# Reordering the values and the transposes of a fused sketch-attention and expert-attention kernel

## The chip, the cores and the metric

The kernel runs on one core of a Trainium2 chip. The metric is the device time of one execution in microseconds. A core has TensorE (PE, the matmuls; PEld are its weight loads), VectorE (DVE), ScalarE (ACT), GpSimd (POOL) and SyncE (SP, here only a DMA queue).

## The reference

Two blocks, one after the other. The first is a linear attention with 4 heads over 1088 positions and 4 batches; its output, 4 x 32 wide, is the input `x` (4, 1088, 128) of the second:

```python
phi(x) = outer(S1 @ x, S2 @ x)              # 8 * 8 = 64 features per head
x = (phi(q) @ (phi(k).T @ v)) / (phi(q) @ phi(k).sum() + 1e-6)

logits = x @ w_gate                          # 4 experts, the best 2 are kept, softmax over them
for e in range(4):
    q, k, v = x @ wq[e], x @ wk[e], x @ wv[e]         # 64 wide
    a = softmax(causal(q @ k.T / 8))                  # 1088 x 1088
    out += gate[:, e] * (a @ v @ wo[e])               # 0 for the experts not kept
```

Everything is fp32.

## The kernel before, in words

Per batch, `prepare` computes `x` and projects it: sketches (`kps`, `qps`), products on GpSimd (`kp`, `qp`), `kv`, turned features (`tq`), numerators (`num`), turned `x` (`tx`), values with gate logits (`vg`), queries and keys (`qk`, `qkt`). It is cut into pieces. Those of batch b+1 wait in the queue `fill` and are let out a few at a time by `spend` between the steps of batch b, so that PE has other work there. The fourth batch has no fill.

The expert attention of a batch goes by steps. One step is one tile of 128 query rows with one pair of experts: tile i (0 to 7) has 128(i+1) keys, and the pair g is 0 or 1. Two tiles 2p and 2p+1 of one pair are a group; its two steps are called its first and its second here. The last 64 query rows, with both pairs at once, are the last unit (`scores_last`). The order of groups is p = 0, 1, 2, 3, each with both pairs, then the last unit; in the fourth batch p = 3, the last unit, then p = 2, 1, 0.

A step does this. `scores` (L391) writes the scores of the two experts and adds the causal mask (L394); for more than 512 keys each expert takes a whole buffer of `ps_sc` (two buffers of two banks). VectorE takes the maxima (L401, or L398 for both at once), ScalarE the exponentials with their sums (L377). `turns_of` gives a list of jobs, each of which turns up to four 128 x 128 blocks of the exponentials on PE (L446) into one bank and copies it to `aT` (`evacuate`, every third copy on VectorE, L71, the others on ScalarE, L73). A list for tile i has ceil((i+1)/2) jobs.

At a group's end `gates` makes 1/sum on VectorE (L458, L459) and `rb`, gate weight times 1/sum, on GpSimd (L462); later PE turns `rb` (`rt`, L469) and ScalarE copies it to `rs`. The values (`av`, L511; L548 in the last unit) need the group's whole `aT`. `av` times `rs` gives `yT` (L521), and when both pairs are done `output` projects it (`po`, L567) and stores it.

PE's order is the order in which the program is written (`manual_schedule` for PE). The orders of the other engines come from a scheduler. Of the eight PSUM banks `ps_sc` has four, `ps_tp` three (turns, `rt`, `po`, all of `prepare`, one small score tile of the last unit), and `ps_o` one (`av`, and the other small score tile). A pool's buffers are given out in turn, so a tile waits until the one as many places before it has been read.

The main loop runs step n so: scores of its tile; the turns of the tile before, with fill between; at the last gap the oldest entry of `later`; then, if the tile before closed a group, `close`: gates, and the first half of that group's values. The second half, with `rt` ahead, is an entry of `later` and so falls in the next step:

```python
turn = gates(name, z, gw[:, 2 * p : 2 * p + 2, 2 * g : 2 * g + 2], 256)
values(0, p + 1)
def rest():
    rs = turn()
    values(p + 1, 2 * p + 2)
```

In the last unit's step the turns come first, then its scores and three doses of fill, then `close` of the group before.

## Time and profile before

| what | number |
|---|---|
| median of 3 runs | 468.26 us (466.32 to 468.36) |
| the profiled execution | 466.51 us, span of its core 464.7 us |
| busy: PE, PEld | 406.0 us, 266.7 us |
| busy: DVE, ACT, POOL | 232.7 us, 224.5 us, 63.4 us |
| chain that ended last | PE 68%, DVE 16%, ACT 9% |
| granted TensorE clock, mean | 0.986 of full speed |

The span runs from the first to the last instruction of the core. Matmuls are pipelined and their ends are modelled, so the busy time of PE is not PE at its peak. "Idle before" is the idle time of an engine just before a group of instructions, with the instruction that ended it.

### The profile page before, as it was taken

To read this page: it belongs to the slowest core of one execution; us is meant where nothing else is said; L and a number is where in the kernel's file an instruction comes from. 1 tells how busy PE (TensorE), PEld (TensorE's weight loads), DVE (VectorE), ACT (ScalarE), POOL (GpSimd) and SP (SyncE) were. 2 spreads that over 40 slices of the span, in tenths; PEclk is the share of its full clock that TensorE was granted. 3 is DMA by queue.
4 is the path that set the end of the run, shared out by engine and by line. 5 is a ranking of instruction groups with operands and counts; after the bars stand their busy time and mean duration, and the time that the engine had idled before them with its cause. 6 is when DMAs were issued, how large, how long until landed. Compare 5 with 4: busy or idle time off the path is not lost.

```text
span 464.7 us, 8178 instructions
## 1 busy us (share of the span) xinstructions
PE 406.0 (87%) x3264; PEld 266.7 (57%) x3264; DVE 232.7 (50%) x495; ACT 224.5 (48%) x564; POOL 63.4 (14%) x99
## 2 busy tenths in 40 slices
PE   0579989998996999999898999989899899699995
PEld 0574665764553676675554676765455465366653
DVE  3673754654553355545636344555364535434542
ACT  1124554545454345545645445545445545435652
POOL 4230172000000036000000027000000000000100
PEclk9999999999998999999999999999999999899997
DMA  7450031000000000000000000000000000000000
GB/s 209 126 146 1 1 105 54 1 11 1 11 2 1 13 4 13 0 13 2 0 13 1 1 16 13 2 11 1 1 12 1 0 13 4 0 1 16 1 13 23
DMA packets 11510, 9.98 MB, mean 21 GB/s; under 512 B 3792, under 2 KB 10448, under 8 KB 11472
## 3 DMA queue, kind: packets, MB, share of 16 engines
q1 hardware_dynamic: 9280, 8.92, 6.7%
q10 hardware_dynamic: 2064, 0.53, 0.5%
q8 instruction: 25, 0.41, 0.4%
q14 instruction: 13, 0.11, 0.1%
q0 software_dynamic: 128, 0.01, 0.0%
HBM read 7.23 MB, written 2.23 MB: 20 GB/s over the span
## 4 chain that ended last, share of the span: by engine, by line
PE 68%; DVE 16%; ACT 9%; issue 3%; DMA 2%; POOL 1%; ACTq 0%; DVEq 0%
PE sc L391 16%; PE av L511 15%; PE tp L446 10%; DVE mx L401 6%; ACT a L377 5%; PE qk L313 4%; PE po L567 3%; PE num L288 3%; PE sc L394 3%; PE av L548 2%; DVE aT L71 2%; PE vg L325 2%; DVE mx L429 2%; PE kps L236 2%; PE rt L469 2%
## 5 line engine op out<-in xcount | busy, mean ns | idle before, releaser
L73 ACT COPY aT<-tp 128x512 f32<-128x512 f32 (+1 forms) x119 | 63.5, 542 | 127.6 <-PE tp L446 127.5
L377 ACT ACTIVATE a<-sc,mx 128x1024 f32<-128x1024 f32 (+7 forms) x136 | 103.0, 763 | 36.8 <-DVE mx L431 14.2
L446 PE MATMUL tp<-ident,a 128*128 128x128 f32 (+1 forms) x648 | 98.6, 277 | 5.7 <-DVE vt L71 1.8
L401 DVE TENSOR_REDUCE mx<-sc 128x1 f32<-128x640 f32 (+3 forms) x64 | 62.6, 1019 | 69.8 <-PE sc L394 69.7
L511 PE MATMUL av<-aT,vt 128*64 128x256 f32 (+1 forms) x640 | 80.6, 381 | 13.1 <-ACT a L377 11.6
L446 PEld LDWEIGHTS tp<-ident,a 128*128 128x128 f32 (+1 forms) x648 | 70.8, 141 | 22.4 <-issue 7.4
L391 PE MATMUL sc<-qkT 64*128 64x512 f32 (+3 forms) x384 | 82.6, 518 | 0.0
L462 POOL TENSOR_TENSOR rb<-gw,r 128x256 f32<-128x256 f32 (+1 forms) x36 | 21.2, 588 | 362.7 <-DVE r L459 289.5
L511 PEld LDWEIGHTS av<-aT,vt 128*64 128x64 f32 x640 | 42.0, 140 | 40.3 <-ACT a L377 12.8
L391 PEld LDWEIGHTS sc<-qkT 64*128 64x128 f32 x384 | 33.1, 185 | 36.3 <-issue 31.4
L71 DVE COPY aT<-tp 128x512 f32<-128x512 f32 (+2 forms) x61 | 38.7, 640 | 14.6 <-PE tp L446 14.5
L398 DVE TENSOR_REDUCE mx<-sc 128x2 f32<-128x256 f32 (+3 forms) x32 | 26.3, 822 | 30.3 <-PE sc L394 29.8
L313 PE MATMUL qk<-xT,wqk 128*128 128x512 f32 x64 | 32.4, 603 | 0.8 <-ACT xT L73 0.8
L377 ACT ACTIVATION_READ_ACCUMULATOR a<-sc,mx 128x1 f32 x136 | 27.4, 201 | 0.0
L325 PE MATMUL vg<-wvg,xT 128*128 128x260 f32 (+1 forms) x72 | 21.9, 400 | 4.8 <-DVE aT L71 2.2
L236 PE MATMUL kps<-SKW,kT 128*128 128x128 f32 x72 | 12.1, 320 | 14.2 <-DVE SKW L163 14.2
L521 DVE TENSOR_TENSOR yT<-av,rs 128x256 f32<-128x256 f32 x32 | 13.4, 420 | 21.1 <-PE av L511 20.9
L567 PE MATMUL po<-wo,yT 128*128 128x128 f32 (+1 forms) x144 | 21.7, 293 | 2.3 <-DVE aT L71 1.1
L394 PEld LDWEIGHTS <-identb 128*128 128x128 bf16 x128 | 7.3, 97 | 28.1 <-issue 26.2
L567 PEld LDWEIGHTS po<-wo,yT 128*128 128x128 f32 (+1 forms) x144 | 18.2, 192 | 6.3 <-DVE aT L71 1.9
L236 PEld LDWEIGHTS kps<-SKW,kT 128*128 128x128 f32 x72 | 10.6, 226 | 15.1 <-DVE SKW L163 14.2
L469 PE MATMUL rt<-ident,rb 128*128 128x128 f32 x68 | 13.7, 279 | 5.5 <-DVE aT L71 2.4
(117 smaller groups left out, 409.0 us busy)
## 6 DMA issues: line engine op xcount, KB each, us to landing
kin<-in_k_dram SPq DMA_DIRECT2D x4, 544.0 KB, 3.7
qin<-in_q_dram SPq DMA_DIRECT2D x4, 544.0 KB, 6.0
vin<-in_v_dram SPq DMA_DIRECT2D x16, 128.0 KB, 2.8
out_dram<-ob SPq DMA_DIRECT2D x16, 128.0 KB, 1.8
wqk<-in_moe_wq_dram ACTq DMA_DIRECT2D x1, 128.0 KB, 5.1
wqk<-in_moe_wk_dram ACTq DMA_DIRECT2D x1, 128.0 KB, 5.1
wvg<-in_moe_wv_dram ACTq DMA_DIRECT2D x1, 128.0 KB, 3.3
wo<-in_moe_wo_dram ACTq DMA_DIRECT2D x1, 128.0 KB
```

The costliest lines, as they stand in the source:

```text
L71: nc.vector.tensor_copy(out_, in_)
L73: nc.scalar.copy(out_, in_)
L236: nc.tensor.matmul(t[:, w * (j - j0) : w * (j - j0) + w], xT_[:, 128 * j : 128 * j + 128], SKW.rearrange("p s x h r -> p (s x h r)"), star ...
L313: nc.tensor.matmul(t, wt(a), xT[:, 512 * c : 512 * c + 512], start=True, stop=True)
L325: nc.tensor.matmul(t[0:m, 0 : E * HD + E], xT[:, 128 * j : 128 * j + m], wvg, start=True, stop=True)
L377: nc.scalar.activation(out=dst, in_=src, func=ACTF.Exp, bias=mx, accum_out=z)
L391: nc.tensor.matmul(sc[e][:, c0:c1], qk[rows, g, 128 * i : 128 * i + 128], qk[rows, NG + g, c0:c1], start=True, stop=(c1 < n))
L398: nc.vector.tensor_reduce(mx, t[:, :, 0:n], axis=AX.X, op=ALU.max, negate=True)
L401: nc.vector.tensor_reduce(mx[:, e : e + 1], sc[e][:, 0:n], axis=AX.X, op=ALU.max, negate=True)
L446: nc.tensor.transpose(tp[0:nk, k - k0, :], ats[e][:, 128 * j : 128 * j + nk], ident)
L511: nc.tensor.matmul(av[HD * e : HD * e + HD, lo:256], vt[:, j, c : c + HD], aT[:, 2 * j + e, lo:256], start=(j == 0), stop=(j == 2 * p + 1))
L567: nc.tensor.matmul(po[0:nq, DM * x : DM * x + DM], yT[:, g, 128 * x : 128 * x + nq], wo_sb[:, g], start=(g == 0), stop=(g == NG - 1))
```

## The change

It does three things.

1. `ps_o` is gone and `ps_tp` has four banks. `av` and both small score tiles of the last unit come out of it.
2. The values of a group are one piece, issued right behind the scores of the next group's second tile (in the last unit's step: behind its scores). The turn of the gates, `rt`, is a job of the next group's first step, after the turns and `output`.
3. Where a tile has more than two jobs of turns (tiles 4 to 7), the first half is issued at the end of the tile's own step, and only the rest in the next step.

The doses of fill differ with it: 1.4 shares in a group's first step, 0.6 in its second and 2.4 in the last unit's, of 19 shares a batch, where each step had one of 16 (and 1.5 in the last unit's). The core of the diff:

```diff
-    ps_tp = ctx.enter_context(tc.tile_pool(name="ps_tp", bufs=3, space=bass.MemoryType.PSUM))
-    ps_o = ctx.enter_context(tc.tile_pool(name="ps_o", bufs=1, space=bass.MemoryType.PSUM))
+    ps_tp = ctx.enter_context(tc.tile_pool(name="ps_tp", bufs=4, space=bass.MemoryType.PSUM))
...
-        ext = [ps_o.tile([128, 512], F32, tag="o", name=f"ext{b}_0"), ps_tp.tile([128, 512], F32, tag="tp", name=f"ext{b}_1")]
+        ext = [ps_tp.tile([128, 512], F32, tag="tp", name=f"ext{b}_{e}") for e in range(2)]
...
-                def values(j0, j1, p=p, g=g, aT=aT, yT=yT, name=name, box=[]):
-                    if j0 == 0:
-                        box[:] = [ps_o.tile([128, 512], F32, tag="o", name=f"av{name}")]
-                    av = box[0]
-                    for j in range(j0, j1):
+                def values(rs, p=p, g=g, aT=aT, yT=yT, name=name):
+                    av = ps_tp.tile([128, 512], F32, tag="tp", name=f"av{name}")
+                    for j in range(2 * p + 2):
...
-                def close(p=p, g=g, yT=yT, z=z, name=name, values=values):
-                    turn = gates(name, z, gw[:, 2 * p : 2 * p + 2, 2 * g : 2 * g + 2], 256)
-                    values(0, p + 1)
-                    def rest():
-                        rs = turn()
-                        values(p + 1, 2 * p + 2)
-                        av = values.__defaults__[-1][0]
-                        nc.vector.tensor_tensor(out=yT[:, g], in0=av[:, 0:256], in1=rs, op=ALU.mult)
-                        if g == NG - 1:
-                            later.append(lambda: output(b, p, yT))
-                    later.append(rest)
+                    nc.vector.tensor_tensor(out=yT[:, g], in0=av[:, 0:256], in1=rs, op=ALU.mult)
+                    return (lambda: output(b, p, yT)) if g == NG - 1 else None
+
+                def close(p=p, g=g, z=z, name=name, values=values):
+                    return gates(name, z, gw[:, 2 * p : 2 * p + 2, 2 * g : 2 * g + 2], 256), values
...
-            share = sum(c for c, _ in fill) / (2 * NJ)
...
+            share = sum(c for c, _ in fill) / 19.0
+            for n, (kind, make, turned, close) in enumerate(units(b, *now)):
+                jobs, turns = turns, []
+                if done:
+                    jobs.append(done)
+                    done = None
...
+                    if kind == "A":
+                        box = []
+                        jobs.append(lambda gate_turn=gate_turn, box=box: box.append(gate_turn()))
+                if kind == "L":
+                    for f in jobs:
+                        f()
+                    values = gate_turn()
                     ats = make()
...
+                    done = values()
+                    group = None
+                    for _ in range(4):
+                        spend(share * 2.4 / 4)
+                else:
+                    ats = make()
+                    if kind == "B" and group:
+                        done = group()
+                        group = None
+                    us = share * (1.4 if kind == "A" else 0.6)
+                    gaps = max(len(jobs), 2)
+                    for s in range(gaps):
+                        if s < len(jobs):
+                            jobs[s]()
+                        spend(us / gaps)
+                    if kind == "A" and group:
+                        group = box[0]
...
+                turns = turned(ats)
+                if len(turns) > 2 and kind != "L":
+                    for f in turns[: len(turns) // 2]:
+                        f()
+                    turns = turns[len(turns) // 2 :]
+                if close:
+                    group = close()
```

`kind` is "A" for a group's first step, "B" for its second and "L" for the last unit's.

In the instructions the names end in a number of the buffer; ahead of it stand the batch (0 to 3), the tile or group, the pair, and for `tp` the first block. Line numbers of the changed kernel are one smaller, three at the values, and up to 16 further down. The first place is PE in the last unit of the second batch. Before:

```order
L313 MATMUL qk2_2_0_2336<-xT2_1355,wqk_163 128x512
L414 MATMUL sc1_8_0_2339<-qkT1_371 64x512 x2
L414 MATMUL sc1_8_1_2340<-qkT1_371 64x512 x2
...
L414 MATMUL ext1_0_2341<-qkT1_371 64x64 x2
L414 MATMUL ext1_1_2342<-qkT1_371 64x64 x2
...
L313 MATMUL qk2_1_0_2377<-xT2_1355,wqk_163 128x512
L313 MATMUL qk2_3_0_2380<-xT2_1355,wqk_163 128x512
L511 MATMUL av1_3_1_2388<-aT1_3_1_2155,vt1_160 64x256 x8
L391 MATMUL sc2_0_0_2405<-qkT2_1356 128x128 x2
```

And in the change:

```order
L468 MATMUL rt1_3_1_2307<-ident_139,rb1_3_1_2290 128x128 x2
L413 MATMUL sc1_8_0_2312<-qkT1_368 64x512 x2
L413 MATMUL sc1_8_1_2313<-qkT1_368 64x512 x2
...
L413 MATMUL ext1_0_2314<-qkT1_368 64x64 x2
L413 MATMUL ext1_1_2315<-qkT1_368 64x64 x2
...
L508 MATMUL av1_3_1_2350<-aT1_3_1_2163,vt1_157 64x256 x14
L508 MATMUL av1_3_1_2350<-aT1_3_1_2163,vt1_157 64x128 x2
L324 MATMUL vg2_6_2368<-wvg_161,xT2_1371 128x260
L324 MATMUL vg2_7_2371<-wvg_161,xT2_1371 128x260
L324 MATMUL vg2_8_2374<-wvg_161,xT2_1371 64x260
L312 MATMUL qk2_0_0_2396<-xT2_1371,wqk_160 128x512
```

The whole values of the group before, and its turned gates, stand in this step now; the fill is behind them.

The second place is PE in a group's first step, tile 6 of the second pair, from its scores to those of tile 7. Before:

```order
L391 MATMUL sc1_6_1_1_2158<-qkT1_371 128x384
...
L446 MATMUL tp1_3_0_1_0_2172<-ident_142,a1_7_0_0_2106 128x128
...
L446 MATMUL tp1_3_0_1_8_2187<-ident_142,a1_7_0_0_2106 128x128
...
L567 MATMUL po1_2_2196<-wo_165,yT1_2_1791 128x128 x4
...
L446 MATMUL tp1_3_0_1_12_2204<-ident_142,a1_7_0_0_2106 128x128
...
L511 MATMUL av1_3_0_2218<-aT1_3_0_2045,vt1_160 64x256 x8
L391 MATMUL sc1_7_1_0_2227<-qkT1_371 128x512
```

And in the change:

```order
L390 MATMUL sc1_6_1_1_2166<-qkT1_368 128x384
...
L445 MATMUL tp1_3_0_1_8_2180<-ident_139,a1_7_0_0_2113 128x128
...
L324 MATMUL vg2_1_2186<-wvg_161,xT2_1371 128x260
L445 MATMUL tp1_3_0_1_12_2189<-ident_139,a1_7_0_0_2113 128x128
...
L324 MATMUL vg2_2_2195<-wvg_161,xT2_1371 128x260
L551 MATMUL po1_2_2198<-wo_162,yT1_2_1793 128x128 x4
L324 MATMUL vg2_3_2206<-wvg_161,xT2_1371 128x260
L468 MATMUL rt1_3_0_2209<-ident_139,rb1_3_0_2161 128x128 x2
L324 MATMUL vg2_4_2214<-wvg_161,xT2_1371 128x260
L445 MATMUL tp1_3_1_0_0_2217<-ident_139,a1_6_1_0_2174 128x128
...
L390 MATMUL sc1_7_1_0_2229<-qkT1_368 128x512
```

The step turns the second half of tile 7 of the first pair, then the first half of its own tile (`tp1_3_1_0` from `a1_6_1`); the half of the values is gone from it.

The third place is GpSimd around the sketch products of the second batch, where `kp2` and `qp2` belong to the fill. Before:

```order
L462 TENSOR_TENSOR rb1_0_0_1553<-gw1_372,r1_0_0_1550 128x256
L249 TENSOR_TENSOR kp2_1612<-kab2_1542 128x9x64 x4
L462 TENSOR_TENSOR rb1_0_1_1635<-gw1_372,r1_0_1_1632 128x256
L249 TENSOR_TENSOR qp2_1673<-qab2_1617 128x9x64 x4
L462 TENSOR_TENSOR rb1_1_0_1753<-gw1_372,r1_1_0_1750 128x256
```

And in the change:

```order
L461 TENSOR_TENSOR rb1_0_0_1498<-gw1_369,r1_0_0_1495 128x256
L248 TENSOR_TENSOR kp2_1614<-kab2_1544 128x9x64
L461 TENSOR_TENSOR rb1_0_1_1592<-gw1_369,r1_0_1_1589 128x256
L248 TENSOR_TENSOR kp2_1614<-kab2_1544 128x9x64 x3
L248 TENSOR_TENSOR qp2_1670<-qab2_1619 128x9x64 x4
L461 TENSOR_TENSOR rb1_1_0_1678<-gw1_369,r1_1_0_1675 128x256
```

One `rb` stands behind the first product now, the next behind the other seven.

## Rows read from the trace of the kernel before

**Rows 1.** The page, busy time, share of the span and instructions of each engine.

```profile
PE 406.0 (87%) x3264; PEld 266.7 (57%) x3264; DVE 232.7 (50%) x495; ACT 224.5 (48%) x564; POOL 63.4 (14%) x99
```

**Rows 2.** Waits of PE: who waited for whom, us in total, times, longest.

```profile
PE av L511 <- ACT a L377: 11.6, 4, 4.1
PE rt L469 <- DVE aT L71: 2.4, 5, 0.5
...
PE vg L325 <- DVE aT L71: 2.2, 4, 0.7
PE rt L469 <- ACT aT L73: 1.8, 2, 1.1
PE tp L446 <- DVE vt L71: 1.8, 2, 0.9
PE vg L325 <- DVE vt L71: 1.8, 2, 0.9
...
PE po L567 <- DVE aT L71: 1.1, 2, 0.6
...
PE tq L279 <- ACT qpT L73: 1.0, 1, 1.0
...
PE tp L446 <- ACT qkT L73: 0.9, 2, 0.4
...
PE po L567 <- ACT aT L73: 0.7, 2, 0.5
```

**Rows 3.** Timeline, second batch's last unit: start, us, instructions, idle before and releaser.

```profile
250.00 0.25 PE L424 MATMUL ext<-cmask,identb 128*64 128x64 bf16 x4
...
253.89 0.30 ACT L377 ACTIVATE a<-ext,mx 128x64 f32<-128x64 f32 x1
...
254.34 1.95 PE L511 MATMUL av<-aT,vt 128*64 128x256 f32 x16 [2.17 <-ACT a L377]
...
255.27 0.32 ACT L377 ACTIVATE a<-ext,mx 128x64 f32<-128x64 f32 x1
```

**Rows 4.** Fourth batch's last unit: timeline; then a window: length, busy PE, clock, DMA.

```profile
403.77 3.62 PE L511 MATMUL av<-aT,vt 128*64 128x256 f32 x16 [4.09 <-ACT a L377]
403.70:407.40 3.70, 3.63 (x18) 0.54 0.00 0
```

**Rows 5.** Timeline, second batch, from an output projection through the step of tile 7.

```profile
232.08 1.16 PE L567 MATMUL po<-wo,yT 128*128 128x128 f32 x8
...
233.07 0.60 PE L446 MATMUL tp<-ident,a 128*128 128x128 f32 x4
...
233.51 0.60 PE L325 MATMUL vg<-wvg,xT 128*128 128x260 f32 x2
...
234.04 1.95 PE L511 MATMUL av<-aT,vt 128*64 128x256 f32 x16
...
235.92 1.99 PE L391 MATMUL sc<-qkT 64*128 64x512 f32 x8
...
237.96 0.61 PE L446 MATMUL tp<-ident,a 128*128 128x128 f32 x4
238.10 2.36 DVE L401 TENSOR_REDUCE mx<-sc 128x1 f32<-128x1024 f32 x2 [3.71 <-PE sc L394]
...
240.38 0.42 DVE L71 COPY vt<-vg 128x260 f32<-128x260 f32 x1
...
240.85 0.70 PE L325 MATMUL vg<-wvg,xT 128*128 128x260 f32 x2 [0.90 <-DVE vt L71]
...
242.00 0.21 ACT L377 ACTIVATION_READ_ACCUMULATOR a<-sc,mx 128x1 f32 x1
```

**Rows 6.** Timeline, second batch: sketch products, the gate weights behind them, and their turn.

```profile
169.82 4.59 POOL L249 TENSOR_TENSOR kp<-kab 128x576 f32<-128x576 f32 x4 [9.45 <-DVE r L458]
...
174.36 0.61 POOL L462 TENSOR_TENSOR rb<-gw,r 128x256 f32<-128x256 f32 x1
...
175.03 0.44 PE L469 MATMUL rt<-ident,rb 128*128 128x128 f32 x2 [0.52 <-POOL rb L462]
```

More of the change, by code (lines that the diff above doesn't have):

```diff
@@ L477 @@
     fill = collections.deque()
-    later = collections.deque()
     debt = [0.0]
@@ L538, in last_unit, with values @@
         yT = p2.tile([128, NG, 256], F32, tag="yT", name=f"yT{b}_8")
-        def close():
-            turn = gates(f"{b}_8", z, gw8[:, None, :], 128)
-            av = ps_o.tile([128, 512], F32, tag="o", name=f"av{b}_8")
-            def half(g):
+        def values(rs):
+            av = ps_tp.tile([128, 512], F32, tag="tp", name=f"av{b}_8")
+            for g in range(NG):
                 for j in range(NJ):
@@ L549, in half @@
                                          aT[0:m, 2 * j + e, 64 * g : 64 * g + 64], start=(j == 0), stop=(j == NJ - 1))
[L550 to L560 removed]
+            nc.vector.tensor_tensor(out=yT[:, :, 0:64], in0=av[:, 0:128].rearrange("p (g s) -> p g s", g=NG),
+                                    in1=rs[:, 0:128].rearrange("p (g s) -> p g s", g=NG), op=ALU.mult)
+            return lambda: output(b, NJ // 2, yT)
+        return ("L", lambda: scores_last(b, qk, z[:, 0]), lambda ats: turns_of(f"{b}_8", NJ - 1, ats, aT, 0),
+                lambda: (gates(f"{b}_8", z, gw8[:, None, :], 128), values))
     def output(b, p, yT):
@@ L579 @@
                 f()
-        turns, after = [], None
+        turns, group, done = [], None, None
         for b in range(B):
@@ L584, with gate_turn @@
             need = len(pieces)
-            share = sum(c for c, _ in fill) / (2 * NJ)
-            for n, (make, turned, close, last) in enumerate(units(b, *now)):
-                ready = list(later)
-                later.clear()
-                if not last:
-                    ats = make()
-                gaps = max(len(turns), 2)
-                for s in range(gaps):
-                    if ready and s == gaps - 1:
-                        ready.pop(0)()
-                    if s < len(turns):
-                        turns[s]()
-                    spend(share / gaps)
+            share = sum(c for c, _ in fill) / 19.0
[4 more added lines that the diff above has]
+                    done = None
+                if group and kind != "B":
+                    to_gate, values = group
+                    def gate_turn(to_gate=to_gate, values=values):
+                        rs = to_gate()
+                        return lambda: values(rs)
+                    if kind == "A":
[5 more added lines that the diff above has]
+                    values = gate_turn()
+                    ats = make()
+                    done = values()
[15 more added lines that the diff above has]
+                        group = box[0]
                 if n == 0 and b == 0:
@@ L600 @@
                         spend(1.0)
-                if n == 2 * NJ // 2 - 2:
+                if n == NJ - 2:
                     while len(fill) > need:
                         spend(1.0)
-                for f in ready:
-                    f()
-                if last:
-                    ats = make()
-                    for _ in range(3):
-                        spend(share / 2)
-                if after:
-                    after()
-                turns, after = turned(ats), close
+                turns = turned(ats)
[5 more added lines that the diff above has]
+                    group = close()
             while fill:
@@ L616 @@
             now, own = coming, rest
-        for f in turns:
-            f()
-        while later:
-            later.popleft()()
-        after()
-        while later:
-            later.popleft()()
+        to_gate, values = group
+        for f in turns + ([done] if done else []):
+            f()
+        values(to_gate())()
 _INS = ['q', 'k', 'v', 'S1', 'S2', 'moe_w_gate', 'moe_wq', 'moe_wk', 'moe_wv', 'moe_wo']
```

16 lines of the change are left out of this document (3 added, 13 removed).

## The prediction

> **What bounds the kernel now.** I read the page first, then the waits of TensorE, then the timeline where those waits lie. TensorE (PE) is busy for 406.0 us, 87% of the span; no other engine passes 50% [rows 1]. So PE's own work sets the time, and what can be won is time in which PE stands. The list of PE's waits names two sorts in the body of the program [rows 2]. One is four waits of the values matmuls for an exponential, 11.6 us. The other is a wait for a copy out of PSUM, many times: the nine rows below the first, 22 waits, 13.7 us together. PE's order is written out by hand and kept, so whatever stands behind a waiting matmul stands too.
>
> The four long waits are one place, the last unit of each batch [rows 3]. Its 64-column scores go to a bank of the one-bank pool, and the next user of that bank is the first half of the group's values. The last mask is written at 250.0, the exponential of that bank runs at 253.89, and the values start at 254.34, after 2.17 us of nothing. [...]
>
> The waits for copies are the three-bank pool [rows 5]: VectorE spends 2.36 us on two maxima before it copies anything (its copy at 240.38), and the fill matmul that wants the bank starts at 240.85, 0.90 us late.
>
> **How large a wait is.** The idle column counts from a modelled end. Four transpositions at 233.07 last 0.60 us by their row, yet the next matmul starts 0.44 us after them [rows 5]. I therefore add 0.17 us to each old wait, since my new waits are counted from start to start. [...] By the idle column alone the sum below would be 7.3 us instead of 11.9.
>
> **Edit 1: the one-bank pool goes, the values of a group come in one piece.** The last unit's values now take the fourth bank after the gate transposition and the two small score tiles, and that bank was copied out long before. Gone: 11.6 us, 4 x 0.17, and twice 3.62 - 1.95 = 1.67 us of slow clock, 15.6 us. What is late next: the fill tiles behind the values take the banks of the two small score tiles. These are read until 254.2 and 255.6, that is 4.0 and 5.4 us behind the last mask [rows 3]. In front of them stand now both halves of the values, about 3.6 us (16 matmuls 1.88 from start to start [rows 5], the second half a little less) and one or two fill tiles of 0.5 to 0.9. I take a rest of 0.1, 0.8 and 0.2 us in the first three batches. The fourth has no fill: its next scores want the large score banks, the second of them free at some 255.2, 5.1 us after the mask (just ahead of the small exponential at 255.27), so 1.5 us. Together 2.6; bounds 1 and 7 (the old 11.6 halved). Net **-13.0 us**. The instructions are the same, so PE's busy work does not change.
>
> **Edit 2: four banks, half of a large tile's transposes in its own step.** Large tiles are 4 to 7, two pairs each: 16 steps of a first tile (4 or 6) and 16 of a second (5 or 7) in the four batches. A tile's exponentials are ready about 3.7 us after its last mask at 1024 keys (4.25 in rows 5, from 237.96 to 242.21, some 0.5 of it a copy to `aT` between the two exponentials). With the maxima at 2.36/1024 us a key that is 3.4 at 896 keys, 3.1 at 768 and 2.8 at 640. The own-step half must wait for that; before, PE never waited for the exponentials of the tile it had just scored. Against it stands the PE work put in front, priced from start to start in rows 5: four transposes 0.44, a value projection 0.53, an output projection 0.99, the values of a whole group 3.6 (tiles 6, 7) or 2.7.
>
> In the step of a group's second tile the whole values stand in front: 2.7 or 3.6 plus 0.7 to 1.8 against 3.1 (768 keys) or 3.7. These 16 steps are nearly covered; 0.2 each, 3.2. In the step of the first tile there is only the other half of the earlier tile, the gate transposition, sometimes an output projection, and fill. In the second batch: tile 4 of the first pair has 0.44 + 0.44 + 0.44 + 0.3 + 0.44 = 2.0 against 2.8, wait 0.8. Tile 6 of the first pair has 2.0 against 3.4, 1.4. Tile 6 of the second pair has 4.4, enough, but its fifth tile (the output projection) needs the first one's bank, whose copy stands on VectorE behind the maxima (2.1 + 0.7) while PE is there after 2.0: 0.9. Tile 4 of the second pair: 0.2. That is 3.3; in the same way 2.6, 2.3 and 3.2 in the first, third and fourth, 11.4 in all. New waits 14.6, bounds 5 (all covered) and 40 (below). Old copies' waits: 13.7 + 22 x 0.17 = 17.4. Net **-2.8 us**.
>
> [...]
>
> **Edit 3: the gate transposition stands a step earlier.** It was in the second step after its group's close, behind two score tiles; now it is in the first, behind one. It reads `rb`, made by GpSimd, and GpSimd also makes the sketch products: four in 4.59 us, with `rb` straight behind at 174.36 and PE 0.52 us late [rows 6]. In the second batch one product, then `rb`, then three and four more and the next `rb`. From the last key sketch on PE has 2.6 us of work to the first gate transposition. `rb` comes after 1.6 (a copy and an addition of 0.4 each by the copy in rows 5, and as much again for what stands ahead of them in their queues), 1.2 for the product, 0.6 and 0.1: 0.95 late. The last query sketch stands behind that gate. From it on PE has 5.5 (its own end, scores 1.0, turns 0.9, `kv` 2.2, output projection 1.0), GpSimd 2.0 + 4.6 + 0.7 = 7.3: 1.8 late. By the same count 0.55 in the first batch, 1.3 in the third, none in the fourth. New 4.6, bounds 1.5 and 12; old 0.52 + 0.17. Net **+3.9 us**.
>
> Output stores from SyncE move by at most a step and nobody waits for them; the loads stay. I cost both at nothing.
>
> **Sum.** -13.0 - 2.8 + 3.9 = -11.9, from the profiled execution's 466.5 us to 454.6. That execution lies 1.75 us under the median of the three runs, 468.26, so against the median I say **456 us**.
>
> **Rivals.**
> 1. *All cover holds.* The fourth bank removes the copies' waits and the first-tile waits shrink to those of the second tile: 11.4 less, 444 to 449. For it: VectorE and ScalarE are half idle. Against: in the fourth batch nothing fills the steps. Chance 0.15.
> 2. *The gate takes the long wait's place.* If `rb` comes behind all products of a batch, PE stands some 4.1 us in three batches and the clock falls as in rows 4: 3 x (4.1 + 1.7) - 4.6 = +12.8, 468 us. For it: rows 6, where products and `rb` share a queue. Against: in the new order of GpSimd one, four or seven products stand ahead of an `rb`, never all eight, and PE has the work counted above in front. Chance 0.12.
> 3. *Slower: four banks set the wait, not the cover.* In a first-tile step PE gets through four tiles, about 2.0 us, and stands if the copy of the first is on ScalarE behind both exponentials, 3.4 + 0.6: 2.1 us, then the fill behind it is too late to cover anything. In all 16 steps that is 16 x 2.1 = 34 instead of 11.4, 478 us. It decides from 10 of the 16 steps on (10 x 1.4 = 14 us lifts 456 to 470). For it: the copies of rows 2 are of this kind, and the long values piece holds a fourth bank. Against: two thirds of these copies can run before the first exponential, which starts 1.3 us after the scores. Chance 0.09.
> That the change does not do what it says is excluded by its order of instructions. The forecast, 449 to 462, has 0.64.
>
> **Numbers.** About 0.5% (2.3 us) is what a measurement of this kernel can tell from no change. Faster by more: 0.64, rival 1, and a third of rival 2, 0.82; the same: two thirds of rival 2 and a little of rival 3, 0.10; slower 0.08. The range, 446 to 467, leaves out the low part of rival 1 (0.06), the upper half of rival 2 and rival 3.
>
> **What would show it.** The wait of the values for an exponential falls from 11.6 us to nothing; the granted clock stays whole at the last unit of the first and fourth batches. A new row appears, transposes waiting for `a` on ScalarE, of 5 to 14 us, and the gate transposition's wait for GpSimd rises from 0.5 to 3 to 5. Wrong would be the copies' waits at 14 us or more, or a new idle stretch of 4 us with a slow clock behind it.

## The result and the profile after

The changed kernel takes **437.2 us** (median of 4 runs, 433.5 to 437.6) against 468.3 us (466.3 to 470.4): ratio 0.9322, 95% interval 0.9266 to 0.9377. It is faster, as forecast, but by 31 us where 12 were forecast, and 437 lies below the range of 446 to 467. Some executions ran slower at a lower granted clock, as two of the change with the gate turn late, 443.1 and 443.9 us at 0.969 and 0.964 against 435.8 and 439.0 at 0.986 and 0.979; the ratios below leave such executions out, and that kernel's trace is of the one at 443.1.

The profiled execution took 433.48 us with a span of 430.9. The first line of its page answers to [rows 1]:

```profile
PE 394.8 (92%) x3264; PEld 272.0 (63%) x3264; DVE 234.2 (54%) x495; ACT 225.3 (52%) x564; POOL 63.4 (15%) x99
```

Its waits of PE answer to [rows 2] (who waited for whom, us in total, times, longest):

```profile
PE tp L445 <- ACT a L376: 4.8, 9, 1.0
PE rt L468 <- POOL rb L461: 3.8, 5, 1.3
...
PE po L551 <- ACT aT L72: 0.8, 1, 0.8
PE sc L390 <- ACT a L376: 0.8, 2, 0.5
...
PE tq L278 <- ACT aT L72: 0.8, 1, 0.8
...
PE vg L324 <- DVE vt L70: 0.5, 1, 0.5
```

The row of the values that waited 11.6 us for an exponential is gone. Of the copy rows some 3.8 us are left, in eight waits. Behind the wait for the first load, 14.2 us in both kernels, two rows that were forecast stand on top: transpositions that wait for their own tile's exponentials, and the gate turn that waits for GpSimd.

The timeline of the second batch's last unit, which answers to [rows 3]:

```profile
231.42 0.25 PE L423 MATMUL ext<-cmask,identb 128*64 128x64 bf16 x4
231.50 3.44 PE L508 MATMUL av<-aT,vt 128*64 128x256 f32 x32
234.87 0.70 PE L324 MATMUL vg<-wvg,xT 128*128 128x260 f32 x2
235.76 1.29 PE L324 MATMUL vg<-wvg,xT 128*128 128x260 f32 x4 [0.19 <-ACT a L376]
```

The values start 0.08 us behind the masks; the third fill tile waits 0.19 us for a small score tile. In the fourth batch (answering to [rows 4]) the wait is at the next scores, as forecast, and is 0.53 and 0.27 us; a window over that unit shows the clock whole, as it is in the first batch's last unit too, 1.00 from 40.50 to 429.50 us (length, busy PE, clock, DMA):

```profile
372.96 3.44 PE L508 MATMUL av<-aT,vt 128*64 128x256 f32 x32
376.92 1.12 PE L390 MATMUL sc<-qkT 64*128 64x512 f32 x2 [0.53 <-ACT a L376]
378.31 1.12 PE L390 MATMUL sc<-qkT 64*128 64x512 f32 x4 [0.27 <-ACT a L376]
...
365.50:376.00 10.50, 10.50 (x108) 1.00 0.00 0
```

PE's sum of idle time fell from 58.7 to 36.1 us (the span less PE's busy time), 22.6 of the 33.8 us by which the span fell. The other 11.2 are PE's busy time, though the instructions are the same. The clock explains little of it: before, PE was busy for 6.8 us at a granted clock of 0.50 in two last units (and for 2.8 us at the very end); in the change's profiled execution it was so for 6.8 us in the first batch's preparation (see below). Counted from each matmul's start to the next one's, waits included, the turns take 11.6 us less than before, the values 9.7 and the small score tiles 8.7 (the old wait stood behind those). So the busy column holds delays that the idle column does not show.

### The profile page after: what moved, and what is told of

The parts are those of the page before. It is cut to its first block, busy times and chain, and to the rows that moved or that the text cites. A ratio compares the mean times of both kernels' runs of the same rounds, so it can differ in the third digit from the quotient of the medians.

```text
span 430.9 us, 8172 instructions
## 1 busy us (share of the span) xinstructions
PE 394.8 (92%) x3264; PEld 272.0 (63%) x3264; DVE 234.2 (54%) x495; ACT 225.3 (52%) x564; POOL 63.4 (15%) x99
## 4 chain that ended last, share of the span: by engine, by line
PE 74%; ACT 9%; DVE 8%; issue 3%; POOL 3%; DMA 2%; ACTq 0%; POOLq 0%; DVEq 0%
PE sc L390 17%; PE tp L445 14%; PE av L508 13%; PE qk L312 7%; ACT a L376 7%; PE num L287 3%; PE sc L393 3%; PE po L551 3%; PE kps L235 2%; PE vg L324 2%; PE tq L278 2%; PE av L537 2%; PE sc L413 2%; DVE mx L400 2%; PE rt L468 1%
## 5 line engine op out<-in xcount | busy, mean ns | idle before, releaser
L445 PE MATMUL tp<-ident,a 128*128 128x128 f32 (+1 forms) x648 | 95.1, 277 | 6.3 <-ACT a L376 4.8
L390 PE MATMUL sc<-qkT 64*128 64x512 f32 (+3 forms) x384 | 80.9, 518 | 0.8 <-ACT a L376 0.8
L508 PE MATMUL av<-aT,vt 128*64 128x256 f32 (+1 forms) x640 | 69.2, 363 | 0.0
L508 PEld LDWEIGHTS av<-aT,vt 128*64 128x64 f32 x640 | 42.9, 137 | 21.7 <-issue 0.2
L390 PEld LDWEIGHTS sc<-qkT 64*128 64x128 f32 x384 | 32.2, 185 | 31.3 <-issue 26.2
L70 DVE COPY aT<-tp 128x512 f32<-128x512 f32 (+2 forms) x58 | 37.8, 652 | 16.5 <-PE tp L445 15.9
L235 PE MATMUL kps<-SKW,kT 128*128 128x128 f32 x72 | 11.7, 317 | 14.2 <-DVE SKW L162 14.2
L551 PE MATMUL po<-wo,yT 128*128 128x128 f32 (+1 forms) x144 | 20.5, 282 | 1.3 <-ACT aT L72 0.8
L235 PEld LDWEIGHTS kps<-SKW,kT 128*128 128x128 f32 x72 | 10.6, 226 | 14.5 <-DVE SKW L162 14.2
L248 POOL TENSOR_TENSOR kp<-kab 128x576 f32<-128x576 f32 x13 | 15.5, 1221 | 24.9 <-DVE kab L241 21.6
```

The costliest lines, as they stand in the source:

```text
L70: nc.vector.tensor_copy(out_, in_)
L235: nc.tensor.matmul(t[:, w * (j - j0) : w * (j - j0) + w], xT_[:, 128 * j : 128 * j + 128], SKW.rearrange("p s x h r -> p (s x h r)"), star ...
L390: nc.tensor.matmul(sc[e][:, c0:c1], qk[rows, g, 128 * i : 128 * i + 128], qk[rows, NG + g, c0:c1], start=True, stop=(c1 < n))
L445: nc.tensor.transpose(tp[0:nk, k - k0, :], ats[e][:, 128 * j : 128 * j + nk], ident)
L508: nc.tensor.matmul(av[HD * e : HD * e + HD, lo:256], vt[:, j, c : c + HD], aT[:, 2 * j + e, lo:256], start=(j == 0), stop=(j == 2 * p + 1))
L551: nc.tensor.matmul(po[0:nq, DM * x : DM * x + DM], yT[:, g, 128 * x : 128 * x + nq], wo_sb[:, g], start=(g == 0), stop=(g == NG - 1))
```

## The experiments

Each run differs by the edit named from the kernel named with it. "The change" is the changed kernel, 437.2 us. Ratios are to the kernel before, with their 95% intervals.

### The last unit, mended alone

The kernel before, with both small score tiles from the three-bank pool and the first half of the values ahead of the fill:

```diff
-        ext = [ps_o.tile([128, 512], F32, tag="o", name=f"ext{b}_0"), ps_tp.tile([128, 512], F32, tag="tp", name=f"ext{b}_1")]
+        ext = [ps_tp.tile([128, 512], F32, tag="tp", name=f"ext{b}_{e}") for e in range(2)]
...
                     ats = make()
+                    if after:
+                        after()
+                        after = None
```

> The kernel before with the last unit alone mended: both small score tiles come from the three-bank pool and the first half of the values stands ahead of the fill; everything else as before. If my first term was right (11.6 us of waits, 0.7 of their modelled ends, 3.4 of slow clock, less some 2 us that the fill behind now waits for a small tile's bank), it runs in 453 to 458 us, and the copies' waits stay at 12 to 15 us. If the last unit is where the whole unforeseen gain lies (the stall's slow clock reaching further than I priced), it runs in 437 to 445.

Measured 463.3 us, 0.9897 (0.9859 to 0.9934): 5 us, neither case. Its waits of PE say why:

```profile
PE sc L391 <- ACT a L377: 4.3, 3, 2.0
PE qk L313 <- ACT a L377: 2.6, 2, 1.3
```

Half the values is too little work behind these scores; the wait moves to the fill and to the next scores, 6.9 of the old 11.6 us.

### Is it the bank or the order?

Three runs: the change without its own-step half; the change with three banks and the fourth for the values alone; and both edits together.

```diff
-                if len(turns) > 2 and kind != "L":
+                if False:
```

```diff
-    ps_tp = ctx.enter_context(tc.tile_pool(name="ps_tp", bufs=4, space=bass.MemoryType.PSUM))
+    ps_tp = ctx.enter_context(tc.tile_pool(name="ps_tp", bufs=3, space=bass.MemoryType.PSUM))
+    ps_o = ctx.enter_context(tc.tile_pool(name="ps_o", bufs=1, space=bass.MemoryType.PSUM))
...
-                    av = ps_tp.tile([128, 512], F32, tag="tp", name=f"av{name}")
+                    av = ps_o.tile([128, 512], F32, tag="o", name=f"av{name}")
```

> The changed kernel with all transposes of a tile in the next tile's step, as before the change; four banks, values in one piece and the gate's turn stay. Theory A (own-step half: copies leave the time in which VectorE and ScalarE make the softmax): the copies' waits come back to 10 us or more, the transposes' wait for the exponentials (4.8 us) goes, and the time is 443 to 452. Theory B (the fourth bank alone ends the copies' waits): copies' waits stay under 5 us, and with 4.8 us of own-step waits gone the time is 431 to 437.

> The changed kernel with three banks for turns, fill, gate turns, outputs and the small score tiles, and the fourth reserved for the values (as before the change); order of PE unchanged. Theory B (fourth bank): copies' waits come back to 8 to 14 us and the time is 446 to 452. Theory A (order, not banks): it loses under 5 us, 437 to 442, the copies' waits at 3 to 7 us.

> All transposes in the next step and three banks with a fourth reserved for the values: both of the run's parents in one, so it gives the price of the own-step half without the shared fourth bank. If the two effects add (14.4 us for the bank, 4.4 us for the own-step half), the time is 445 to 449. If the own-step half pays under three banks because it takes copies out of the softmax (Theory A), the time is 452 to 460 and the copies' waits 14 us or more.

| | four shared banks | three and one |
|---|---|---|
| half in its own step | 437.2 (the change) | 451.6, 0.9660 (0.9608 to 0.9712) |
| all in the next step | 432.8, 0.9233 (0.9178 to 0.9288) | 445.5, 0.9507 (0.9468 to 0.9545) |

The effects nearly add: the shared fourth bank is worth 12.7 to 14.4 us, the own-step half costs 4.4 to 6.1. So Theory B holds, and the own-step half is a loss that the rest of the change pays for. The worth of the bank is net of a slow clock in the first preparation: from 27 to 30 us it is 0.50 in the two kernels with four shared banks, and 1.00 in the change with three and one (see below). From the waits of PE with all turns in the next step and three banks:

```profile
PE rt L469 <- POOL rb L462: 3.4, 5, 1.3
PE tp L446 <- ACT aT L73: 2.4, 6, 1.0
PE vg L325 <- DVE aT L71: 1.8, 3, 0.8
PE kv L266 <- DVE qab L242: 1.6, 1, 1.6
```

The row for `tp` and ScalarE's `aT` is a copy wait of the old kind, and it is absent with four banks. How little the idle column tells is seen here too: from the start of each `tp` matmul to the start of the next matmul, summed over all 648, the trace has 93.9 us with three banks and 80.5 with four.

### The doses of fill

The change with even doses; the three-and-one kernel above with even doses.

```diff
-            share = sum(c for c, _ in fill) / 19.0
+            share = sum(c for c, _ in fill) / 17.5
...
-                        spend(share * 2.4 / 4)
+                        spend(share * 1.5 / 4)
...
-                    us = share * (1.4 if kind == "A" else 0.6)
+                    us = share * 1.0
```

> The changed kernel with the fill shared evenly: one share in every step and 1.5 in the last unit's, of 17.5, where the change has 1.4, 0.6 and 2.4 of 19. Theory A (the extra fill in a group's first step is the cover that kept the own-step waits at 4.8 us where I had forecast 14.6): transposes' wait for exponentials rises to 8 to 15 us and the time to 440 to 448. Rival (the second step's long values leave fill no use there, but the first step needs none either): 435 to 439, waits of 4 to 6 us.

> As the run with all transposes in the next step and three plus one banks, with the fill shared evenly, 1, 1 and 1.5 of 17.5, nearly as before the change. If the uneven doses save the unexplained 11 to 12 us, the time is 453 to 458; if the values' place does, 442 to 449.

Measured 434.4 us, 0.9272 (0.9220 to 0.9325), and 448.1 us, 0.9551 (0.9516 to 0.9585). The change lost nothing by even doses (2.8 us less), and its transpositions then waited 3.4 us for exponentials, not more than 4.8; so the extra fill is not what kept the own-step waits low. Without the own-step half the uneven doses are worth 2.6 us. Both differences are about the size of what a comparison can tell.

### Where the values stand

Four kernels with all turns in the next step move the values. With four banks, whole at the end of the group's first step, behind the gate turn:

```diff
-                        jobs.append(lambda gate_turn=gate_turn, box=box: box.append(gate_turn()))
+                        jobs.append(lambda gate_turn=gate_turn, box=box: box.append(gate_turn()()))
...
-                        done = group()
-                        group = None
...
-                        group = box[0]
+                        done, group = box[0], None
```

> As the run with all transposes in the next step, with the values put at the end of a group's first step, right behind the gate turn and ahead of the second tile's scores (before the change half of them stood there). Theory C (the long values behind the second tile's scores are what covers that tile's softmax, and so the release of the score banks): scores wait for exponentials 6 us or more, the time is 438 to 446. Rival (where the values stand does not matter once no transpose waits for its own tile): 430 to 436, the scores' wait under 3 us.

Its ratio is 1.0076 (1.0027 to 1.0126), 472 us: some 39 us lost against 432.8, and a little slower than the kernel before. Its waits of PE:

```profile
PE rt L468 <- POOL rb L461: 10.8, 8, 3.2
PE tp L445 <- ACT a L376: 10.2, 12, 1.3
PE sc L390 <- ACT a L376: 6.8, 12, 1.1
```

The values all stand in the first step now; the second is shorter than its softmax, and the gate turn is met before GpSimd is done. The sign of Theory C came (6.8 us of waits of the scores, where it asked for 6 or more), but its time, 438 to 446, did not: the waits for the gate's product and of the turns for their exponentials grew by more (3.8 to 10.8 and 1.2 to 10.2 us).

With three and one banks, whole behind the turns of the second step (the values' call moves from ahead of the jobs to behind them):

```diff
-                        done = group()
-                        group = None
...
+                    elif kind == "B" and group:
+                        done, group = group(), None
```

> As the run with all transposes in the next step and three plus one banks, with the whole values of a group at the end of the second step, behind the turns and the fill, instead of between the scores and the turns. If the values' place between scores and turns is what saves the 11 to 12 us that neither the last unit, the fourth bank nor the gate accounts for (it keeps PE off the banks while VectorE makes the maxima), the time is 454 to 460 and the waits for copies rise from 13.5 us to 20 or more. If the whole piece or the doses of fill save it, 443 to 449.

Measured 444.1 us, 0.9457 (0.9421 to 0.9493): within the second step the place does not matter. Cut in two again, as before the change, the first half at the end of the first step:

```diff
                     if kind == "A" and group:
-                        group = box[0]
+                        values(None, 0)
+                        group = lambda values=values, rs=box[0]: values(rs, 1)
```

> As the run with all transposes in the next step and three plus one banks, with each group's values cut in two again: the first half at the end of the first step, the second behind the second tile's scores (before the change they stood so, the second half somewhat later). If the first half in the first step is what costs the unexplained 11 to 12 us (the second step, with half the values, gets shorter than its softmax, and the first half waits for copies): 453 to 458. If the cut costs nothing by itself: 444 to 448.

Measured 459.1 us, 0.9801 (0.9743 to 0.9860): the cut, with one half back in the first step, costs 13.6 us. The idle column explains only part: 43.1 us in 58 waits against 39.8 in 47, 5.2 us more with 0.17 for each wait. The timelines of one group, first in two halves, then whole:

```profile
201.93 1.52 PE L511 MATMUL av<-aT,vt 128*64 128x256 f32 x12
203.38 1.56 PE L391 MATMUL sc<-qkT 64*128 64x512 f32 x8
...
205.08 1.30 PE L511 MATMUL av<-aT,vt 128*64 128x256 f32 x12
206.32 0.44 PE L446 MATMUL tp<-ident,a 128*128 128x128 f32 x2
```

```profile
200.23 2.60 PE L509 MATMUL av<-aT,vt 128*64 128x256 f32 x24
202.76 1.31 PE L446 MATMUL tp<-ident,a 128*128 128x128 f32 x10
```

From start to start the halves take 1.45 and 1.24 us, the whole 2.53: the cut itself costs 0.16 us a group with no wait in sight, 4.1 us over all values matmuls (83.0 against 78.9). The second half is the shorter because four of its twelve matmuls have 128 columns. By the same count the turns take 5.8 us more and the scores 3.8, waits included; what costs that beyond the waits listed I could not place.

### What the last unit is worth

Two kernels price it from the changed order. First the stall is put back: the three-and-one kernel with the first small score tile in the values' bank.

```diff
-        ext = [ps_tp.tile([128, 512], F32, tag="tp", name=f"ext{b}_{e}") for e in range(2)]
+        ext = [ps_o.tile([128, 512], F32, tag="o", name=f"ext{b}_0"), ps_tp.tile([128, 512], F32, tag="tp", name=f"ext{b}_1")]
```

> As the run with all transposes in the next step and three plus one banks, with the first small score tile of the last unit put back into the one bank of the values, so that the values of the group before wait for its exponential as they did before the change. My first term (11.6 us of waits, 0.7 of modelled ends, 3.4 of slow clock, against some 2 us of what then no longer waits): 457 to 461, against 445.5 without the stall, the values' wait 11 us or more. If the stall was worth only what mending it in the kernel before gave (5.2 us): 449 to 453.

Measured 465.2 us, 0.9935 (0.9902 to 0.9969): 19.7 us slower than 445.5, above both cases: here no fill stands ahead of the values, so all four batches wait the full time. The waits, and the timeline in the first batch:

```profile
PE av L509 <- ACT a L377: 16.4, 4, 4.1
```

```profile
137.31 0.25 PE L424 MATMUL ext<-cmask,identb 128*64 128x64 bf16 x4
141.65 5.04 PE L509 MATMUL av<-aT,vt 128*64 128x256 f32 x30 [4.09 <-ACT a L377]
```

Each wait is 4.1 us, and 30 matmuls behind one take 5.04 where 32 take 3.44 in the change, at a granted clock of 0.56 over the first 3.4 us: [rows 4] again.

Then the order before in nearly everything but the last unit: the kernel with two halves, with even doses and the gate turn in the second step.

```diff
                     if kind == "B" and group:
-                        done = group()
+                        to_gate, values = group
+                        rs = to_gate()
+                        done = values(rs, 1)
...
                     if kind == "A" and group:
-                        group = box[0]
+                        group[1](None, 0)
```

> As the run with two halves (three plus one banks, all transposes in the next step), with even doses of fill and the gate turn in the second step: the order before in all but the last unit, whose values stand whole behind its scores. If the last unit is worth my first term (13 to 14 us), it runs in 453 to 456, and what the whole values then save is the step from here to 445.5. If the cut costs 13.6 us in this order too, on top of the last unit, it runs in 456 to 462. If the halves cost only with uneven doses: 445 to 450.

Measured 454.1 us, 0.9697 (0.9646 to 0.9748): the last unit, with the whole values behind its scores, is worth 14.2 us, as far as the small shifts of the gate turn and the second half in this kernel cost nothing.

A third kernel makes the values one piece in the order before, by a one-line edit, which leaves the last unit's step without them:

```diff
-                    values(0, p + 1)
...
-                        values(p + 1, 2 * p + 2)
+                        values(0, 2 * p + 2)
```

> The kernel before with one edit: the first half of a group's values no longer stands at the close of the group but goes with the second half, one piece right behind the gate turn in the second step; three plus one banks, doses of fill and turns as before. It takes the values out of the last unit's step, so that their wait (11.6 us and its slow clock, 15.6 by my first term) goes as well, or becomes a wait of the next scores. If one piece is worth 8 us or more beside that: 441 to 448. If it is worth nothing beside it: 451 to 456. If the last unit's wait only moves to the next scores, as when I mended its banks alone: 458 to 464.

Measured 468.4 us, 1.0001 (0.9969 to 1.0032). The wait changed its name and kept its size:

```profile
PE sc L391 <- ACT a L377: 11.5, 6, 3.8
```

That falls beyond all three cases: one piece gains nothing in this order. The trace shows where the gain goes. From start to start the values take 10.0 us less than before, but the scores 5.7, the turns 3.3 and the projections to queries and keys 3.0 more; and behind the last units' waits the granted clock is 0.50 for 17.0 us, where it was so for 6.8. So the 13.6 us above belong to that order of steps, and are not a price of the cut in any order.

### The gate turn

The change with the gate turn right ahead of the values; then the same without the own-step half, and with the doses of each step kept in number; then that with even doses.

```diff
-                    if kind == "A":
-                        box = []
-                        jobs.append(lambda gate_turn=gate_turn, box=box: box.append(gate_turn()))
...
-                        done = group()
+                        to_gate, values = group
+                        done = values(to_gate())
```

> The changed kernel with the gate transposition moved from the end of a group's first step to the second step, right ahead of the values (in the last unit's step unchanged). My third term says this edit cost 3.9 us, and the profile of the changed kernel shows 3.8 us of waits for GpSimd's product: those go, and the time falls to 432 to 435. Against: the gate turn was cover for the own-step transposes (0.33 us in each first step), and the copy to the scaled sums stands later on ScalarE, behind the second tile's exponentials, so that the values' product waits and holds its bank: then 437 to 441.

> As the run with all transposes in the next step, with the gate turn moved to the second step, right ahead of the values, and as many doses of fill in each step as before. No transpose waits for its own tile here, so the gate turn covers nothing. If my third term holds (3.8 us of waits for GpSimd that the place of the gate turn alone makes): the waits of the gate turn fall to under 1 us and the time to 428 to 431. Rival (the gate's product is late for any place, or the copy behind the softmax on ScalarE holds the values' bank): 432 to 436.

> The fastest order so far (all transposes in the next step, the gate turn ahead of the values) with the fill shared evenly, 1, 1 and 1.5 of 17.5. The even fill gave 2.8 us on the changed kernel. If it does so by itself, the time is 426 to 428.5. If it only served the gate and the own-step transposes there, which this order no longer has, it is 429 to 432.

The first gave 0.9351 (0.9289 to 0.9414), no gain. Its transpositions now wait at eleven of the 16 first steps of large tiles, where the gate turn, and the dose of fill at its gap, had been work in front of them:

```profile
PE tp L445 <- ACT a L376: 12.3, 16, 1.4
```

The second took 429.9 us, 0.9149 (0.9091 to 0.9207), 2.9 less than with the gate turn early; its wait for GpSimd is 1.1 us instead of 3.8. The third took some 432 us, 0.9236 (0.9150 to 0.9323): even doses do not help here. The 2.9 us are little more than a comparison can tell.

### The clock in the first preparation

Three of the change's four runs lie near 437 us with a mean clock of 0.975, the profiled one at 433.5 with 0.991. Windows of the profiled one, ahead of the first scores:

```profile
26.80:30.20 3.40, 3.40 (x19) 0.50 0.68 198
37.10:40.50 3.40, 3.40 (x5) 0.51 0.00 0
```

I gave PE 20 transpositions of the identity there, written to a score buffer and read by nobody, in the change itself, and in the fastest order (429.9 us); then, in the latter, put the values behind the turns as well.

```diff
+        def keep_busy(n):
+            if first:
+                t = ps_sc.tile([128, 1024], F32, tag="sc", name=f"busy{n}")
+                for _ in range(n):
+                    nc.tensor.transpose(t[:, 0:128], ident, ident)
...
-(2.0, lambda: (kvs(0), kvs(1)))
+(2.0, lambda: (kvs(0), kvs(1), keep_busy(12)))
...
+        tq[0] = (0.5, lambda: (turn_features(0), keep_busy(8)))
```

> The changed kernel itself with the 20 idle transpositions on PE in the first batch's preparation. If its runs at 437 us and its profiled one at 433.5 differ by the half clock there alone, as in the fastest order: 430 to 433 in all runs, mean clock 0.99 or more. If something in its steps costs clock too: 434 to 437.

> The fastest order so far, with 20 transpositions of the identity on PE in the first batch's preparation (12 behind the sketch sums, 8 behind the first turned features), where PE waits for the products; their result is read by nobody. If the half clock behind that wait (0.50 from about 27 us on, for up to 15 us) is what lies between 424.9 and 430 us among runs of one kernel, the clock stays whole there, the mean clock is 0.99 in all runs, and the median is 424 to 426. If the clock falls whatever PE does there, 429 to 432.

> The fastest kernel so far (four banks, all transposes in the next step, gate turn in the second step, PE kept busy in the first preparation) with the whole values behind the turns instead of ahead of them. Under three plus one banks this place gave 1.4 us: 421 to 424 if that holds with four shared banks. If the values, which take a shared bank here, then wait for it or hold it into the next step: 425 to 430.

Measured 430.3 us, 0.9178 (0.9143 to 0.9212), all four runs within 1.4 us, mean clock 0.995 or more; 423.9 us, 0.9042 (0.8989 to 0.9096); and **421.6 us**, 0.9019 (0.8961 to 0.9077), the fastest of all, 16 us below the change. The last step, 2.2 us, is about the size of what a comparison can tell. The timeline of the fastest order without the extra work:

```profile
21.48 2.29 PE L265 MATMUL kv<-vp,kp 128*64 128x33 f32 x70 [0.55 <-DVE kp L248]
24.90 0.30 PE L278 MATMUL tq<-ident,qp 128*128 128x128 f32 x1 [1.14 <-DVE qp L248]
26.55 2.58 PE L278 MATMUL tq<-ident,qp 128*128 128x128 f32 x11 [1.35 <-DVE kT L222]
28.93 2.66 PE L287 MATMUL num<-kvz,qpT 128*128 128x66 f32 x12
```

its windows there,

```profile
24.00:27.00 3.00, 0.75 (x3) 0.78 0.01 3
27.00:30.00 3.00, 3.00 (x16) 0.50 0.73 216
```

and the timeline of the last kernel, with it:

```profile
23.86 1.53 PE L288 MATMUL busy<-ident 128*128 128x128 f32 x12
...
26.72 0.52 PE L278 MATMUL tq<-ident,qp 128*128 128x128 f32 x3 [1.22 <-DVE kT L222]
27.08 1.04 PE L288 MATMUL busy<-ident 128*128 128x128 f32 x8
...
28.82 1.45 PE L293 MATMUL num<-kvz,qpT 128*128 128x66 f32 x12
```

The same twelve numerators take 2.66 us in the one, at a clock of 0.50, and 1.45 in the other, at 1.00 (its window from 27 to 42 us).

## Why the prediction was wrong, step by step

The ledger follows one chain of runs: before (468.3), the last unit alone (454.1), values whole with uneven doses and the gate turn early (445.5), four banks (432.8), the change (437.2). The second link is split by the runs on doses (2.6) and gate (2.9), each little more than noise; the whole values are what is left of it, and no run has them alone. In the traces of this link the values take 4.8 us less and the turns 3.4.

| term | forecast | measured |
|---|---|---|
| Edit 1, last unit's stall and slow clock | -13.0 | -14.2 |
| Edit 1, values whole elsewhere | 0 | -8.9 |
| doses of fill | 0 | -2.6 |
| Edit 2, the fourth bank | -17.4 | -12.7 |
| Edit 2, own-step half | +14.6 | +4.4 |
| Edit 3, gate turn | +3.9 | +2.9 |
| sum | -11.9 | -31.1 |

**What held.** The last unit is right in mechanism, and in size where the whole values stand behind its scores: 14.2 us, though mending it alone gave 5.0 and putting its stall back cost 19.7. The slow clock that the term counts twice is in the trace of before in the first batch too, where the values waited 4.09 us, and not in the second with its shorter wait; these are the windows of the two (length, busy PE, clock, DMA):

```profile
144.30:148.00 3.70, 3.63 (x18) 0.54 0.00 0
254.30:258.00 3.70, 3.66 (x31) 1.00 0.00 0
```

The gate turn's wait is right; its price is 2.9 us without the own-step half, and with it the run with the gate turn late showed none. The signs that I named came but for one: no wait of the values, a whole clock in the last unit, 3.8 us for GpSimd (3 to 5); the 4.8 us for the exponentials are just under the 5 to 14.

**The step that failed most: new waits of 14.6 us in Edit 2.** The second steps' part, 3.2, did not appear at all. In the first steps I counted 2.6, 3.3, 2.3 and 3.2 us by batch; the change's waits for exponentials there are 0.5, 1.7, 0.3 and 1.8, at five steps of 16. Where I had worked it out, in the second batch, one of four waits came: tile 6 of the first pair was to wait 1.4 and waited 1.02 and 0.65. For its tile 4 I gave 0.8, and the timeline of the change has 0.78, but at a copy:

```profile
176.30 0.28 PE L393 MATMUL sc<-cmask,identb 128*128 128x128 bf16 x2
...
178.90 0.66 PE L278 MATMUL tq<-ident,qp 128*128 128x128 f32 x4 [0.78 <-ACT aT L72]
179.39 0.84 PE L445 MATMUL tp<-ident,a 128*128 128x128 f32 x4
```

That match is luck. With all turns in the next step the same matmul waits as long for the same copy (its waits of PE):

```profile
PE tq L278 <- ACT aT L72: 0.8, 1, 0.8
```

So part of the waiting is the first step being short, whatever PE does in it, and I charged it to the own-step half. Taking the half away gave back 4.4 us, and 6.1 with three banks. What else kept the waits low stays open in part: even doses did not raise them, and the 12.3 us that came with the gate turn late, near my 11.4 for the first steps, say that the gate turn with the dose at its gap covered more than I had counted. That each wait of an own-step transposition costs its full length, as the next scores stand behind it in PE's written order, was my estimate; it was a reason to expect a cost here, and the 4.4 us show one. The sum that I built on it was 10 us too much.

**The step that was missing: "the instructions are the same, so PE's busy work does not change".** I used the long values only as cover for the own-step half and gave their move no price of its own. Cut again, with one half in the first step, they cost 13.6 us with uneven doses; put whole into the first step, 39. Two steps share one pair of score buffers, and what stands in one is missing in the other. What the whole values are worth in the change, 8.9, is a remainder and not a measurement. I also let an uncounted cost pass: in the change PE's rows are 11.2 us less busy, so the busy column held delays. The timelines of the cut group show such a delay, 0.16 us with no idle time shown.

**The fourth bank was 4.7 too high, from two errors that go against each other.** The nine rows that I summed, 13.7 us, were not all: the whole list of before has some 20 us of waits for copies in the body. And the bank brought a cost that I had not looked for. With three banks the sketch sums wait for one (the `kv` row above, 1.6 us; 2.2 before, where they start at 22.60 us); with four they run earlier, at 21.13 us in the change, PE then stands for the products, 1.14 us, and from 27 to 30 us the clock is 0.50. It is 0.50 there in the windows of four kernels with four banks and no extra work: the change, all turns in the next step, and the gate turn late with and without the own-step half. In those of three with three banks, before, the last unit mended alone and the change with three and one, it is 1.00 from 14 to 48 us. Keeping PE busy there gave the change 6.9 us.

Rival 1, 444 to 449, was the nearest, and right that the cover holds; it too had no price for the whole values. Rivals 2 and 3 did not occur: the gate turn's longest wait was 1.3 us and the clock stayed whole there, 1.00 from 40.50 to 429.50 us, and waits for a copy are 3.8 us in all with four banks.

## What to carry to other kernels

A wait that is taken away at one place comes back at the next unless work stands behind it: two edits that took the values' wait away without putting the whole values there gave 5 and 0 us, the one that put the whole values there gave 14. Where steps alternate, ask which step gets longer and which shorter against its own softmax before asking what waits; and sum all rows of a kind of wait, not those at the top. Splitting a change into its parts also showed one that loses: without the own-step half, and with the gate turn late, the same idea ran 7 us faster.

## What the runs showed of the hardware

- The clock fell behind short waits: in the fastest order without the extra work 1.14 and 1.35 us of idle time behind 2.29 us of small matmuls, and from 27 us on the granted clock was 0.50; in the run with all turns in the next step it was 0.50 from 27 to 42 us and still 0.52 from 42 to 45. With 20 matmuls put into these waits it was 1.00 from 20 to 45 us in the change and in the last kernel; in the fastest order it was 1.00 from 21 to 33 us with them, and 0.50 from 36 to 39. The change's profiled execution has two stretches of 3.4 us at 0.50 and 0.51, the first behind waits of 1.14 and 1.34 us, the second behind waits of 0.79 and 0.84. Such waits did not always bring it: before had 2.21, 1.35, 0.88 and 0.85 us in the same preparation, at 1.00 from 14 to 48 us.
- 20 matmuls whose result nobody reads made a kernel 6 to 7 us faster (437.2 to 430.3 us, and 429.9 to 423.9).
- A run of values matmuls costs time at its two ends that no idle column shows. In the two traces of the cut group, pairs of values matmuls with 256 columns start 0.216 us apart; ahead of the scores the last pair takes 0.10 more, ahead of the turns the last pair (128 columns, 0.11 apart) takes 0.10 more too, and the first pair of each run takes 0.05 more.
